# Gate and up by seven products: a pair of position chunks per weight block, even positions ahead of odd ones

## The chip, the cores and the metric

The kernel runs on one core of a Trainium2 chip. The metric is the device time of one execution in microseconds (us), lower is better. A core has five engines that run their own instruction streams and meet at semaphores: TensorE (PE: matmul, with weight loads, PEld, that overlap it), VectorE (DVE), ScalarE (ACT), GpSimd (POOL) and SyncE (SP, which here only issues transfers). Work is in SBUF (128 partitions); matmul results go to PSUM banks of 128 x 512 fp32, eight of them; DMA engines move data to and from HBM.

## The reference

Shapes: S = 2048 positions, D = 640, F = 1536, 32 heads of 20. All in fp32.

```python
xn = layernorm(x)                                    # no scale, no bias
q, k, v = (xn @ wqkv) split in 3, 32 heads of 20
# position s attends to s, s-2, ..., s-14: 8 places, every second one; before the start masked
A  = softmax(q.k * 20**-0.5) @ v, heads joined, @ wo
h  = (xn @ w_gate) * (xn @ w_up)                      # 2048 x 1536
out = x + A * silu(h @ w_down)
```

## The kernel before, in words

**Number format.** Each fp32 operand of a matmul is the sum of a high part (fp32 rounded to the matmul's fp32r format by an ACT copy) and a low part (what is left). A product is three matmuls: high by high, high by low, low by high. The low part comes either from a subtraction on DVE or POOL (`split`, L86 and L87), or without them (`split_dma`): ACT copies the high part (L91), ACT writes its negative into the low tile (L92), and a DMA that POOL issues adds the raw weights from HBM onto it (L93).

**Positions.** Since attention looks at every second position, positions are held as 16 tiles of 128, tiles 0 to 7 the even ones and 8 to 15 the odd ones; four tiles make a chunk of 512. Chunks 0 and 1 are even, 2 and 3 odd. The normalised, transposed input of all four chunks (high and low) stays in SBUF in four buffers `xc`.

**Gate and up.** F is 12 blocks of 128. For block f and chunk ch, `gate_up` runs 5 x 3 = 15 matmuls of 128 x 512 for gate into a PSUM bank `g`, 15 for up into `u` (L102), ACT copies the gate to SBUF (L435), DVE multiplies up by it (L446; the last 11 pairs by ACT and POOL, L448 and L449, when no attention is left on DVE), and SP stores the result to HBM (`h_scr`). There are 48 such pairs. The weight block f+1 is loaded by SP and split while the chunks of block f run.

**Attention.** The 32 heads are five groups of 6 or 7. A unit is a group at one parity, ten in all, group by group. A unit's q, k, v are 8 tiles x 15 matmuls of width 360 or 420 on PE (L327) that ACT moves out of PSUM (L329, L330). Its attention is all DVE work: 4 products q*k for two places at once (L363), 4 sums over a head (L367), softmax (its exponential on ACT, L379), 4 products with v (L388), 3 sums (L396) and a last one (L399). Each is one instruction of 1920 or 2240 elements per partition.

**Order.** The program is written in one order, and each engine runs its instructions in that order. `advance` puts DVE instructions of the attention between the rest: each matmul group on PE gives a credit of its own time (times `PACE`) that the next attention instructions use up. After the front (layernorm, transposes, unit 0, blocks 0 and 1 and unit 1) come units 2 to 9, with 2 to 4 gate/up pairs after each, then blocks 10 and 11 for all chunks, while the attention ends.

**After that.** `out_proj` for 16 tiles, each 30 matmuls of 320 wide (L102 into `q`), while the 12 blocks of `wd` are loaded, summed on DVE and split by ACT and POOL; `trans_o` (L507 and L87, all DVE) prepares each tile. Then the down projection: for 8 pairs of tiles 7 products of 18 matmuls of 320 wide (L646). These are already of the Strassen-Winograd kind: 7 half-size products of sums of quarters instead of 8, and where a result is wanted in two banks, ACT copies the bank to a second one, onto which later matmuls go on adding.

Of the kernel before, what the change touches and what calls it, by code (L numbers as in the profile page):

```python
# [42 lines left out]
PACE = 1.0  # L43
# [8 lines left out]
def kernel(  # L52
# [30 lines left out]

    def split(eng, raw, hi, lo):

        nc.scalar.activation(hi, raw, AF.Copy)  # L86
        eng.tensor_sub(lo, raw, hi.bitcast(F32))  # L87
# [17 lines left out]
    wq_raw, wq = {}, {}  # L105

    def load_wq(g, parts):
        c3 = 3 * GROUPS[g] * DH
        wq_raw[g] = []
        for p in parts:  # L110
            t = st([P, p[-1] - p[0], c3], "wraw", 3)
            for k0, k1 in zip(p, p[1:]):
                nc.sync.dma_start(t[:, k0 - p[0]:k1 - p[0]], wqkv[g][:, k0:k1, :])
                wq_raw[g].append((k0, k1, t[:, k0 - p[0]:k1 - p[0]]))

    def split_wq(g, eng, ks=(0, KD)):
        c3 = 3 * GROUPS[g] * DH
        if g not in wq:
            cp = -(-c3 // 64) * 64
            wq[g] = [st([P, KD, cp], tag, 1, F32R)[:, :, :c3] for tag in ("wqh", "wql")]  # L120
        for k0, k1, t in wq_raw[g]:
            if ks[0] <= k0 < ks[1]:
                if g:
                    split_dma(t, wqkv[g][:, k0:k1, :], wq[g][0][:, k0:k1], wq[g][1][:, k0:k1])
                else:
                    split(eng, t, wq[g][0][:, k0:k1], wq[g][1][:, k0:k1])

    wf_raw, wf = {}, {}

    def load_wf(f):  # L130
        wf_raw[f] = st([P, KD, 2, P], "wraw", 3)
        nc.sync.dma_start(wf_raw[f], wgu[f])

    def split_wf(f, eng, cuts=(0, KD)):
        hi, lo = st([P, KD, 2, P], "wf", 4, F32R), st([P, KD, 2, P], "wf", 4, F32R)
        if f > 1:
            split_dma(wf_raw[f], wgu[f], hi, lo)
        else:
            for k0, k1 in zip(cuts, cuts[1:]):
                split(eng, wf_raw[f][:, k0:k1], hi[:, k0:k1], lo[:, k0:k1])  # L140
        wf[f] = hi, lo


# [13 lines left out]
    load_wq(0, ((0, 1, 2, 3), (3, 4, 5)))  # L157
    load_x(2, 2, xe[:, 0:2])
    load_wf(0)
    xc = st([P, NE, D], "xc", NCH)  # L160
    load_x(4, 4, xc[:, 0:4])
    load_wf(1)
    load_x(8, 4, xc[:, 4:8])
    xd = st([P, 1, D], "o", 1)
    load_x(14, 1, xa[:, 2:3])
    load_x(15, 1, xd)
# [3 lines left out]
    def idle_product(n):  # L170

        nc.tensor.matmul(pt([P, n, P], "q", 4), ident, ident.unsqueeze(1).to_broadcast([P, n, P]), start=True,
                         stop=True)

    for n in (3, 3, 3, 2):
        idle_product(n)
# [3 lines left out]
    o_scr = dr.tile([DIL, NQ, NE, P, QC], F32, name="o_scr")  # L180
    h_scr = dr.tile([NT, P, KF, P], F32, name="h_scr")
    s_scr = dr.tile([NT, P, D], F32, name="s_scr")

    xT = []

    def xT_tile(s):
        if s % TPC == 0:
            y = st([P, 2, KD, CH], "xc", NCH, F32R)
            xT.append((y[:, 0], y[:, 1]))
        hi, lo = xT[s // TPC]  # L190
        c = (s % TPC) * P
        return hi[:, :, c:c + P], lo[:, :, c:c + P]

# [45 lines left out]
    def trans(s, later=False):  # L239
        hi, lo = xT_tile(s)  # L240
        for k0, k1 in ((0, 4), (4, KD)):
            p = pt([P, k1 - k0, P], "q", 4)
# [5 lines left out]
        if not later:  # L248
            low_parts()

# [19 lines left out]
    def spread(s):  # L270

        b = (s - FIRST) // 4
        p = pt([P, NQ, 2, 4], "q", 4)
# [3 lines left out]
    def trans_quarters(s):  # L277
# [3 lines left out]
        y = st([P, KD, P], "ot", 2)  # L281
        nc.vector.transpose(y.rearrange("p k (q i) -> p k q i", i=QB),  # L282
                            xt[s].rearrange("p (q k j) -> p k q j", q=NQ, j=QB))
        hi, lo = xT_tile(s)
        nc.scalar.activation(hi, y, AF.Copy)
        low_parts()
        halves.append(lambda: nc.vector.tensor_sub(lo, y, hi.bitcast(F32)))
# [8 lines left out]
    UN = [(g, r) for g in range(len(GROUPS)) for r in range(DIL)]  # L296
    q_t, kv_t, kv_buf, kv_zero = {}, {}, {}, {}

    def begin_unit(u, zero=True):
        g, r = UN[u]  # L300
        c = GROUPS[g] * DH
        q_t[u] = st([P, NE * CMAX + 32], "q", 2)[:, :NE * c].rearrange("p (i c) -> p i c", c=c)
        if r not in kv_buf:
            kv_buf[r] = st([P, EXT * 2 * CMAX], f"kv{r}", 1)
            kv_zero[r] = 0
        kv_t[u] = kv_buf[r][:, :2 * EXT * c].rearrange("p (a e c) -> p a e c", a=2, c=c)
        if zero:
            zero_front(u)

    def zero_front(u):  # L310
        g, r = UN[u]
        if kv_zero[r] != GROUPS[g]:
            nc.gpsimd.memset(kv_t[u][0:1, :, 0:W - 1, :], 0.0)
            kv_zero[r] = GROUPS[g]
# [3 lines left out]
    def qkv(u, i, runs=ALL_RUNS, at=None, act=None):  # L318
# [3 lines left out]
        p = pt([P, 3 * c], "q", 4)  # L322
        t0 = (i % TPC) * P
        for n, (a, b, k) in enumerate(runs):
            if n == at:
                act()
            nc.tensor.matmul(p, xT[(r * NE + i) // TPC][a][:, k, t0:t0 + P], wq[g][b][:, k], start=n == 0,  # L327
# [94 lines left out]
    def gate_up_half(f, ch, n, p, c=slice(0, CH), **parts):  # L422
        mm3(p[:, c], [([t[:, k, n, :] for t in wf[f]], [t[:, k, c] for t in xT[ch]]) for k in range(KD)], **parts)

    def gate_up(f, ch, between=(), amid=(), part=None):
# [5 lines left out]
        gate_up_half(f, ch, 0, pp[0], c)  # L431
# [4 lines left out]
        for act in between:  # L436
            act()
        share = (c.stop - c.start) / CH
        finish_piece()
        advance(PACE * 3.25 * share)  # L440
        gate_up_half(f, ch, 1, pp[1], c)

        def finish():
            hs = st([P, CH], "hs", 2)
            if running:
                nc.vector.tensor_mul(hs, pp[1], gs)  # L446
            else:
# [286 lines left out]
    for i in range(4):  # L734
        qkv(1, i)
# [173 lines left out]
```

## Time and profile before

| | us |
|---|---|
| runs (median of 3) | 770.22 (769.85 to 770.49) |
| profiled execution, its own time | 770.31 |
| its span in the trace | 768.5 |
| PE busy | 759.9 (99%) |
| DVE busy | 626.8 (82%) |
| ACT busy | 251.2 (33%) |
| POOL busy | 106.4 (14%) |
| bytes by DMA | 104.50 MB, 136 GB/s on average |

The span runs from the first to the last instruction in the trace; the execution's own time holds 1.81 us more. Busy shares are means over stages of unlike kind, so the stages are read apart: the front up to about 60 us, units and gate/up to 546, out projection to 616.4, down projection to the end.

### The profile page before, as it was taken

How to read it: one execution, taken by the hardware profiler on the slowest of the kernel's cores; microseconds unless marked ns; L12 is line 12 of the kernel's file. 1: busy time of each engine (PE TensorE's matmuls, PEld its weight loads, DVE VectorE, ACT ScalarE, POOL GpSimd, SP SyncE). 2: the span in 40 equal slices, each digit the busy share in tenths (PEclk: the TensorE clock that was granted, in tenths of full speed). 3: DMA queues.
4: the chain of work that ended last, by engine and by line, in shares of the span. 5: the costliest groups of instructions: out<-in, count | busy, mean ns of one | idle time of the engine just before them, and what ended most of it. 6: DMA issues, size and time to landing. Idle time of an engine off the chain costs nothing.

```text
span 768.5 us, 10609 instructions
## 1 busy us (share of the span) xinstructions
PE 759.9 (99%) x4192; PEld 700.5 (91%) x4192; DVE 626.8 (82%) x630; ACT 251.2 (33%) x520; POOL 106.4 (14%) x120
## 2 busy tenths in 40 slices
PE   8999999999999999999999999999999999999997
PEld 6989889999898998989889898888999999999997
DVE  6677999898999989989998999960377587777775
ACT  5323342113222132221412122213356554444442
POOL 7201011000100011010100000005377500000000
PEclk9999999999999999999999999999999999999999
DMA  8352185133643436235542422542887465555533
GB/s 327 145 171 87 40 210 118 53 106 104 118 108 84 140 72 135 74 67 150 111 95 86 87 88 66 176 100 72 209 244 209 168 250 183 186 187 185 185 104 137
DMA packets 82423, 104.50 MB, mean 136 GB/s; under 512 B 21101, under 2 KB 61901, under 8 KB 82117
## 3 DMA queue, kind: packets, MB, share of 16 engines
q1 hardware_dynamic: 72544, 84.16, 34.6%
q0 software_dynamic: 4128, 10.55, 8.1%
q10 hardware_dynamic: 5700, 9.11, 4.1%
q8 instruction: 33, 0.54, 0.3%
q14 instruction: 18, 0.14, 0.1%
HBM read 66.38 MB, written 28.31 MB: 123 GB/s over the span
## 4 chain that ended last, share of the span: by engine, by line
PE 93%; DMA 2%; DVE 2%; ACT 1%; ACTq 1%; issue 0%; POOL 0%; SPq 0%; POOLq 0%; DVEq 0%
PE q L327 24%; PE u L102 20%; PE g L102 20%; PE q L646 11%; PE q L102 9%; PE u L646 5%; PE g L646 3%; DMA wraw<-in_wgu 1%; DMA xc<-in_xq 1%; DVE xc L224 1%; ACTq L334 1%; DMA wraw<-in_wqkv 1%; DVE ot L282 0%; DVE stats L200 0%; POOL wql L87 0%
## 5 line engine op out<-in xcount | busy, mean ns | idle before, releaser
L102 PE MATMUL u<-xc,wf 128*128 128x512 f32 (+1 forms) x735 | 171.8, 386 | 0.0
L102 PE MATMUL g<-xc,wf 128*128 128x512 f32 (+1 forms) x735 | 171.8, 385 | 0.0
L102 PEld LDWEIGHTS u<-xc,wf 128*128 128x128 f32 x735 | 136.1, 188 | 27.3
L102 PEld LDWEIGHTS g<-xc,wf 128*128 128x128 f32 x735 | 136.0, 188 | 26.5
L327 PE MATMUL q<-wqh,xc 128*128 128x360 f32 (+1 forms) x800 | 152.9, 334 | 1.3 <-ACT xc L245 1.2
L327 PEld LDWEIGHTS q<-wqh,xc 128*128 128x128 f32 x800 | 138.3, 188 | 3.6 <-ACT xc L245 2.0
L388 DVE TENSOR_TENSOR t<-lg,kv 128x1920 f32<-128x1920 f32 (+1 forms) x40 | 90.8, 2288 | 0.8
L363 DVE TENSOR_TENSOR t<-q,kv 128x1920 f32<-128x1920 f32 (+1 forms) x40 | 90.9, 2287 | 0.5
L367 DVE TENSOR_REDUCE lg<-t 128x96 f32<-128x1920 f32 (+1 forms) x40 | 90.3, 2279 | 0.0
L327 PE MATMUL q<-wql,xc 128*128 128x360 f32 (+1 forms) x400 | 81.8, 334 | 0.0
L435 ACT ACTIVATE gs<-g 128x512 f32<-128x512 f32 x48 | 28.6, 595 | 160.3 <-PE g L102 156.4
L329 ACT ACTIVATE kv<-q 128x240 f32<-128x240 f32 (+1 forms) x80 | 30.9, 386 | 146.2 <-PE q L327 137.8
L327 PEld LDWEIGHTS q<-wql,xc 128*128 128x128 f32 x400 | 69.7, 188 | 0.1
L396 DVE TENSOR_TENSOR t<-t,t 128x1920 f32<-128x1920 f32 (+1 forms) x30 | 68.7, 2289 | 0.7
L646 PE MATMUL q<-xc,wf 128*128 128x320 f32 x432 | 67.3, 310 | 0.0
L646 PEld LDWEIGHTS q<-xc,wf 128*128 128x128 f32 x432 | 64.3, 188 | 0.0
L93 POOL DMA_DIRECT2D wf<-in_wgu x10 | 8.8, 882 | 242.0 <-ACT wf L92 242.0
L102 PE MATMUL q<-wf,wf 128*128 128x320 f32 x156 | 35.6, 310 | 0.0
L330 ACT ACTIVATE q<-q 128x120 f32<-128x120 f32 (+1 forms) x80 | 22.2, 277 | 14.2 <-DMA o_scr<-q 14.2
L102 PEld LDWEIGHTS q<-wf,wf 128*128 128x128 f32 x156 | 26.1, 188 | 0.0
L93 POOL DMA_DIRECT2D wql<-in_wqkv x8 | 10.0, 1246 | 115.1 <-ACT wql L92 114.6
L449 POOL TENSOR_TENSOR hs<-hs,gs 128x512 f32<-128x512 f32 x11 | 14.2, 1293 | 82.9 <-ACT hs L448 47.3
(166 smaller groups left out, 926.1 us busy)
## 6 DMA issues: line engine op xcount, KB each, us to landing
h_scr<-hs SPq DMA_DIRECT2D x48, 256.0 KB, 2.4
wraw<-in_wgu SPq DMA_DIRECT2D x12, 640.0 KB, 5.4
wf<-in_wgu POOLq DMA_DIRECT2D x10, 640.0 KB, 6.6
t<-h_scr SPq DMA_DIRECT2D x8, 768.0 KB, 7.7
hs<-s_scr SPq DMA_DIRECT2D x16, 320.0 KB, 3.5
gs<-in_x SPq DMA_DIRECT2D x16, 320.0 KB, 3.9
wraw<-h_scr SPq DMA_DIRECT2D x12, 384.0 KB, 6.0
out<-q SPq DMA_DIRECT2D x14, 320.0 KB, 2.5
```

What stands on the lines that cost most here:

```text
L93: nc.gpsimd.dma_start(lo, src, accum_op=ALU.add)
L102: nc.tensor.matmul(acc, a, b, start=first and n == 0, stop=last and n == len(runs) - 1)
L327: nc.tensor.matmul(p, xT[(r * NE + i) // TPC][a][:, k, t0:t0 + P], wq[g][b][:, k], start=n == 0, stop=n == len(runs) - 1, skip_group_check ...
L329: nc.scalar.activation(kv_t[u][:, :, W - 1 + i, :], p[:, c:].rearrange("p (a c) -> p a c", a=2), AF.Copy)
L330: nc.scalar.activation(q_t[u][:, i, :], p[:, :c], AF.Copy)
L363: nc.vector.tensor_mul(prods[j], q.rearrange("p i c -> p (i c)").unsqueeze(1).to_broadcast([P, 2, NE * c]), places(0, j))
L367: nc.vector.tensor_reduce(out=lg[:, :, j:j + 2].rearrange("p n a -> p a n"), in_=heads(prods.pop(j)), op=ALU.add, axis=AX.X)
L388: nc.vector.tensor_mul(heads(t), pw, heads(places(1, j)))
L396: nc.vector.tensor_add(acc, acc, t)
L435: nc.scalar.activation(gs, pp[0], AF.Copy)
L449: nc.gpsimd.tensor_mul(hs, hs, gs)
L646: nc.tensor.matmul(p, y[:, i, k], wd_t[name][k][:, l], start=new and r == 0, stop=r == len(runs) - 1, skip_group_check=True)
```

## The change

**Gate and up.** A job is now one block f for both chunks of one parity: 24 jobs, numbered 0 to 23. Four of them (f = 0 and 1 even, f = 11 even and odd) run as before, 15 + 15 matmuls for each chunk. The other 20 run as seven products. The weights of the block are taken as ten 128 x 128 pieces (5 of the inner dimension for gate, 5 for up), the positions as two chunks; four of the five inner pieces form 2 x 2 quarters, and the fifth is added where it belongs. The products have 6, 6, 6, 9, 9, 9 and 9 matmuls of 128 x 512: 54 where there were 60. Three banks hold the results: X (`g`, 2 buffers), V (`u`, 2) and Z (one bank, new, for which `q` gives up one of four). ACT copies X to Z after the first product, and both go on adding.

**Weight sums.** A job needs 16 pieces: 8 of the 10 raw ones and 8 sums. POOL makes the sums (4 instructions of 256 elements per partition) the first time a block is used as seven products, SP stores them to a new `w_scr`, and the second time (the other parity) loads them from there. All 16 pieces are split: 5 copies and 5 negations by ACT, and two DMAs that add, one from the raw weights and one from `w_scr`.

**Input sums.** The sums of the chunks are made once for each parity: for the even one on DVE in the front, for the odd one from HBM (`xt_scr`, to which the front stores the transposed odd tiles, and from which the odd chunks come back into SBUF, too). So only one parity is in SBUF at a time.

**Order.** Units are ordered by parity: 0 to 4 even, 5 to 9 odd. Since a group now comes twice, its qkv weights are loaded and split for every unit. `ORDER` gives the order of jobs (J) and units (U) after the front. A list of events with due times on a modelled PE clock (`later`, `step`, `need`) puts ACT, POOL, DVE and SP instructions between the matmuls.

**End.** `out_proj` of tiles 0 to 7 needs only even units, so the last odd attention may go on into it; `advance(1e9)` stands at s = 6. `trans_o` of tiles 1 to 5 uses ACT and an adding DMA for the low part. The loads, sums and splits of `wd` begin at s = 6, not s = 1.

```diff
-PACE = 1.0
+PACE = 1.02
+MM = 0.2267
+ORDER = "JJJJUJJJUJJUJJUJJUJJUJJUJJUJJJ"
...
+    UN = [(g, r) for r in range(DIL) for g in range(len(GROUPS))]
+    JOBS = [(f, 0, f in (0, 1, KF - 1)) for f in range(KF)]
+    JOBS += [(f, 1, f == KF - 1) for f in (KF - 1, *range(2, KF - 1), 0, 1)]
...
+        def sums():
+            done.add(("raw", i))
+            nc.gpsimd.tensor_sub(b[:, 2:4], a[:, 0:2], a[:, 8:10])
+            nc.gpsimd.tensor_add(a[:, 8:10], a[:, 8:10], a[:, 4:6])
+            nc.gpsimd.tensor_sub(b[:, 0:2], a[:, 8:10], a[:, 0:2])
+            nc.gpsimd.tensor_sub(b[:, 4:6], a[:, 2:4], b[:, 0:2])
+            nc.sync.dma_start(w_scr[f, :, :2], a[:, 8:10])
+            nc.sync.dma_start(w_scr[f, :, 2:], b)
...
+        for n, (k0, k1) in enumerate(cuts):
+            later(CHUNK * 2 * n, lambda k0=k0, k1=k1: high(k0, k1))
+            later(CHUNK * (2 * n + 1), lambda k0=k0, k1=k1: negate(lo[:, k0:k1], hi[:, k0:k1]))
+        later(CHUNK * 3 + 0.1, lambda: nc.gpsimd.dma_start(lo[:, :8], wgu[f, :, :8], accum_op=ALU.add))
+        later(CHUNK * 9 + 0.1, lambda: nc.gpsimd.dma_start(lo[:, 8:], w_scr[f], accum_op=ALU.add))
+        later(CHUNK * 9 + 0.1, lambda: done.add(("wf", i)))
...
+    def prod(p, i, terms, first=False):
+        w = wf[i]
+        runs = [(w[a][:, b], x[c][n]) for a, c in ALL3 for blocks, x in terms for n, b in enumerate(blocks)]
+        for n, (y, x) in enumerate(runs):
+            nc.tensor.matmul(p, y, x, start=first and n == 0, stop=n == len(runs) - 1, skip_group_check=True)
+        return len(runs) * MM
...
+    def strassen(i):
+        f, r, _ = JOBS[i]
+        need(("wf", i), f"xS{r}")
+        x = lambda name: xs(r, name)
+        X, Z, V = pt([P, CH], "g", 2), pt([P, CH], "z", 1), pt([P, CH], "u", 2)
+        t = prod(X, i, [((0, 1), x("B11"))], True)
+        copy(Z, X)
+        step(t)
+        t = prod(V, i, [((8, 9), x("T1"))], True)
+        m5 = copy(st([P, CH], "ot", 2), V)
+        step(t)
+        t = prod(X, i, [((10, 11), x("T2"))])
+        m = copy(st([P, CH], "hs", 2), X)
+        step(t)
+        t = prod(Z, i, [((2, 3), x("B21")), ((6,), x("A5"))])
+        gs = copy(st([P, CH], "gs", 2), Z)
+        step(t)
+        t = prod(X, i, [((12, 13), x("T3")), ((7,), x("B5"))])
+        w = copy(st([P, CH], "ot", 2), X)
+        nc.gpsimd.dma_start(w, m5, accum_op=ALU.add)
+        step(t)
+        t = prod(V, i, [((14, 15), x("B22")), ((6,), x("B5"))])
+        def upper():
+            nc.vector.tensor_add(m, V, m)
+        later(t + 0.3, upper)
+        step(t)
+        t = prod(X, i, [((4, 5), x("T4")), ((7,), x("D5"))])
+        def lower():
+            nc.vector.tensor_mul(gs, X, gs)
+        def both():
+            nc.vector.tensor_mul(m, m, w)
...
+        if s == 6:
+            begin_wd()
             load_wd(0)
+            load_wd(1)
             advance(1e9)
```

Three places of the instruction order follow, each before and in the change. A row gives the line, the operation, output and input by the program's names with a running number, and the shape.

**ACT while a weight block is split.** Before, the two rows of 1280 stand between the gate copies (`gs`) of one block's pairs:

```order
L435 ACTIVATE gs_3053<-g_3036 128x512
L435 ACTIVATE gs_3089<-g_3072 128x512
L91 ACTIVATE wf_3091<-wraw_3034 128x1280
L92 ACTIVATE wf_3092<-wraw_3034 128x1280
L435 ACTIVATE gs_3134<-g_3117 128x512
L435 ACTIVATE gs_3178<-g_3161 128x512
```

In the change, inside one job of seven products (L252 a high part, L155 a negation of the next job's weights, L760 a bank that is copied):

```order
L252 ACTIVATE wf_3041<-wraw_3007 128x512
L760 ACTIVATE ot_3068<-u_3045 128x512
L155 ACTIVATE wf_3042<-wf_3041 128x512
L252 ACTIVATE wf_3041<-wraw_3007 128x256
L760 ACTIVATE hs_3080<-g_3043 128x512
L155 ACTIVATE wf_3042<-wf_3041 128x256
L252 ACTIVATE wf_3041<-wraw_3008 128x384
L760 ACTIVATE gs_3095<-z_3044 128x512
L155 ACTIVATE wf_3042<-wf_3041 128x384
L252 ACTIVATE wf_3041<-wraw_3008 128x384
L155 ACTIVATE wf_3042<-wf_3041 128x384
L760 ACTIVATE ot_3113<-g_3043 128x512
```

The split of the next block is now cut into ten pieces between the copies of the running job, and three of them stand behind the copy of Z (`gs` from `z`), which waits for the fourth product.

**POOL over a few jobs.** Before, POOL has only the adding DMAs there (`wql` the low part of qkv weights, `wf` of gate/up weights):

```order
L313 MEMSET kv_102_753 1x2x980
L93 DMA wql_1689<-in_wqkv 128x3x420
L93 DMA wql_1689<-in_wqkv 128x2x420
L93 DMA wf_1716<-in_wgu 128x1280
L93 DMA wf_2053<-in_wgu 128x1280
```

In the change, two jobs long:

```order
L274 DMA wf_1729<-in_wgu 128x1024
L275 DMA wf_1729<-w_scr 128x1024
L783 DMA ot_1793<-ot_1750 128x512
L228 TENSOR_TENSOR wraw_1797<-wraw_1796 128x256
L229 TENSOR_TENSOR wraw_1796<-wraw_1796 128x256
L230 TENSOR_TENSOR wraw_1797<-wraw_1796 128x256
L231 TENSOR_TENSOR wraw_1797<-wraw_1796,wraw_1797 128x256
L274 DMA wf_1833<-in_wgu 128x1024
L275 DMA wf_1833<-w_scr 128x1024
```

The sums of a job's weights (L228 to L231) now stand directly ahead of the two DMAs of the same job's split (L274, L275), and behind the DMA that adds one product onto another (L783).

**DVE at the end of the attention.** Before, the last attention instruction (L399) stands ahead of the first preparation of a tile for `out_proj` (L507, L87):

```order
L396 TENSOR_TENSOR t_3914<-t_3914,t_3913 128x1920
L399 TENSOR_TENSOR q_3544<-t_3914 128x960
L507 STREAM_TRANSPOSE ot_4205<-wraw_3943 128x640
L87 TENSOR_TENSOR kv_497_4207<-ot_4205,kv_497_4207 128x640
L507 STREAM_TRANSPOSE ot_4266<-o_4210 128x640
```

In the change (L667 and L659 are the lines that were L396 and L388, L670 was L399, L843 was L507):

```order
L667 TENSOR_TENSOR t_4809<-t_4809,t_4808 128x1920
L659 TENSOR_TENSOR t_4808<-lg_4546,kv_109_776 128x1920
L843 STREAM_TRANSPOSE xa_4876<-xa_4772 128x640
L667 TENSOR_TENSOR t_4809<-t_4809,t_4808 128x1920
L659 TENSOR_TENSOR t_4808<-lg_4546,kv_109_776 128x1920
L843 STREAM_TRANSPOSE xa_4921<-xa_4772 128x640
L667 TENSOR_TENSOR t_4809<-t_4809,t_4808 128x1920
L670 TENSOR_TENSOR q_4287<-t_4809 128x960
L843 STREAM_TRANSPOSE ot_5002<-xa_4772 128x640
L126 TENSOR_TENSOR wf_5004<-ot_5002,wf_5004 128x640
```

Transposes for `out_proj` now stand between the attention's last instructions, and the one for tile 6 (`ot_5002`) with its low part behind all of them.

More of the change, by code (lines that the diff above doesn't have):

```diff
@@ L128 @@
[L128 to L141, printed above, removed]
+        cp = -(-c3 // 64) * 64
@@ L469, in gate_up_first @@
             for n in range(2):
-                gate_up_half(f, ch, n, pp[n], slice(0, CH // 2), parts=parts, first=first, last=not first)
+                gate_up_half(i, ch, n, pp[n], slice(0, CH // 2), parts=parts, first=first, last=not first)
             if first:
@@ new lines @@
+    at, u = 2, 2
+    for what in ORDER:
+        if what == "U":
+            unit(u)
+            u += 1
+        else:
+            job(at)
+            at += 1
+    load_o(4, 4, st([P, 4, D], "xa", 4))
+    finish_piece()
+    trans_o(1)
+    n_prod = 7 * NT // 2
+    items, at = [divmod(n, 2) for n in range(2 * KH)], 0
+    for s in range(NT):
+        if s + 2 < AHEAD_O:
+            trans_o(s + 2)
+        elif AHEAD_O <= s + 1 < NT:
+            trans_o(s + 1)
+        if s == 6:
+            begin_wd()
+            load_wd(0)
+            load_wd(1)
+            advance(1e9)
+            load_o(8, 3, st([P, 3, D], "t", 2))
+        if s in (8, 10):
+            load_o(*((11, 3) if s == 8 else (14, 2)), st([P, 3 if s == 8 else 2, D], "t", 2))
+        now = items[at:max(0, (s - 6) * 2 * KH // 8)]
+        at += len(now)
+        for k, part in now:
```

600 lines of the change are left out of this document (425 added, 175 removed).

## The prediction

> **What bounds the kernel now.** I read the page first: busy times, the slices, the chain that ended last.
>
> ```profile
> span 768.5 us, 10609 instructions
> PE 759.9 (99%) x4192; PEld 700.5 (91%) x4192; DVE 626.8 (82%) x630; ACT 251.2 (33%) x520; POOL 106.4 (14%) x120
> ...
> DVE  6677999898999989989998999960377587777775
> ...
> PE 93%; DMA 2%; DVE 2%; ACT 1%; ACTq 1%; issue 0%; POOL 0%; SPq 0%; POOLq 0%; DVEq 0%
> ```
>
> PE is 99% busy and holds 93% of the chain. DVE is nearly full from slice 5 to slice 26, about 86 to 512 us, so a shorter PE stage there may uncover it. Next the busy times by stage (us, PE, PEld, DVE, ACT, POOL, then clock, DMA share, GB/s):
>
> ```profile
> 0.00:60.00 60.00, 55.66 (x299) 48.00 (x300) 42.82 (x125) 22.45 (x60) 20.40 (x42) 1.00 0.60 207
> 60.00:86.50 26.50, 26.50 (x141) 23.97 (x141) 21.36 (x53) 8.94 (x21) 4.02 (x3) 1.00 0.21 70
> 86.50:240.00 153.50, 153.50 (x756) 139.99 (x755) 147.33 (x95) 41.19 (x88) 10.88 (x9) 1.00 0.44 109
> 240.00:400.00 160.00, 160.00 (x802) 143.21 (x801) 150.44 (x92) 39.28 (x82) 10.82 (x10) 1.00 0.44 107
> 546.00:616.40 70.40, 70.40 (x482) 70.40 (x481) 45.23 (x56) 38.71 (x91) 43.06 (x43) 1.00 0.75 210
> 616.40:768.50 152.10, 147.80 (x1008) 147.54 (x1006) 112.38 (x139) 67.62 (x113) 0.00 (x0) 0.99 0.51 179
> ```
>
> From 60 to 616 us PE never waits, at the full clock (1.00). ACT has three quarters of its time free between 86 and 400 us, DMA more than half. So the time is the number of matmuls by what one takes. What one takes, from the timeline and the chain (start, length, rows):
>
> ```profile
> 501.61 3.56 PE L102 MATMUL u<-xc,wf 128*128 128x512 f32 x15
> 505.00 3.56 PE L102 MATMUL g<-xc,wf 128*128 128x512 f32 x15
> ...
> 305.97 19.20 PE q L327 x120
> 545.97 70.39 PE q L102 x480
> 743.08 5.28 PE q L646 x36
> ```
>
> Fifteen 512-wide matmuls repeat every 505.00 - 501.61 = 3.39 to 3.40 us, 0.2267 us each. `out_proj` starts at 545.97.
>
> **What PE saves.** Each of 20 jobs has 54 matmuls for 60: 120 fewer, 120 x 0.2267 = 27.2 us. That holds only if adding products to one bank, or to a bank that ACT has filled, costs PE nothing. The down projection does both already: 36 of its matmuls take 5.28 us, 0.1467 each, like `out_proj` (70.39 / 480 = 0.1467), which does neither. So span 768.5 - 27.2 = 741.3 if nothing new is waited for. A job is 54 x 0.2267 = 12.24 us, and gate/up would end at 545.97 - 27.2 = 518.8. Below, waits are added to that.
>
> **ACT.** Rows for its work on weights and banks:
>
> ```profile
> L435 ACT ACTIVATE gs<-g 128x512 f32<-128x512 f32 x48 | 28.6, 595 | 160.3 <-PE g L102 156.4
> L91 ACT ACTIVATE wf<-wraw x10: 1259/1267/1274, 94.9 to 495.6; 128x1280 fp32r<-128x1280 f32 x10
> ```
>
> A 512-wide copy is 0.60, a 1280-wide 1.27; by the line through them 256 is 0.37 and 384 is 0.48. A job's five copies out of PSUM take 3.0, the ten split pieces 2 x (2 x 0.60 + 0.37 + 2 x 0.48) = 5.1: 8.1 of 12.24 us, so ACT is no bound. The copy X to Z must end before Z is added to, two products (12 matmuls, 2.7 us) later, and the copies of X have at least 9 matmuls (2.0 us) before X is written again; 0.60 fits in each, with one split piece ahead of it too. I take 0; each 0.6 us not covered would cost 20 x 0.6 = 12. The qkv weights are now split for every unit, ten ACT pieces of about 0.5 us each, and stand among the copies out of a job's or a unit's banks, which may start a piece late: I take 2 us in all, 0 to 5.
>
> **(a) The second adding DMA.** It is issued when the last negation is done. In the order of ACT three pieces stand behind the copy of Z, which starts after 6 + 6 + 6 + 9 = 27 matmuls, 6.1 us into the job. So 6.1 + 0.6 + 3 x 0.48 = 8.2 us. The rows for how long such a DMA takes to land:
>
> ```profile
> wf<-in_wgu POOLq DMA_DIRECT2D x10, 640.0 KB, 6.6
> DMA to landing us min/median/max: 6.0/6.6/9.9
> q0 software_dynamic: 4128, 10.55, 8.1%
> ```
>
> 8.2 + 6.6 = 14.8. The next job first reads a low part from the second half in the last two matmuls of its second product (ten matmuls in, 2.27 us): at 12.24 + 2.27 = 14.5 if it follows directly. That is 0.3 us late, and with 6.0 not late, with 9.9 it is 3.6 late. Twelve of the transitions between jobs have no unit between them; at the others a unit's 19.2 us cover it. The bytes by order of the program rise from 104 to 165 MB and those that add from 10.55 MB to some 42, so I put the landing 0.3 us above the median: 0.6 x 12 = 7 us. Bounds 0 and 3.6 x 12 = 43. Landings before ran from 6.0 to 9.9, with the median near the low end, so the value lies near that end.
>
> [...]
>
> **(b) POOL's sums.** Eleven blocks get four 256-wide sums on POOL. Their nearest rows (the 256-wide POOL subtractions of the front; a POOL and a DVE subtraction that met in `out_proj`):
>
> ```profile
> L87 POOL TENSOR_TENSOR wf<-wraw,wf x12: 721/740/1571, 13.5 to 529.1; 128x256 fp32r<-128x256 f32 x10, 128x640 fp32r<-128x640 f32 x2
> L87 DVE TENSOR_TENSOR wf<-ot,wf x13: 824/826/1487, 549.4 to 601.6; 128x640 fp32r<-128x640 f32 x13
> 557.47 0.88 POOL L87 TENSOR_TENSOR xc<-lg,xc 128x320 fp32r<-128x320 f32 x1
> 557.54 1.49 DVE L87 TENSOR_TENSOR wf<-ot,wf 128x640 fp32r<-128x640 f32 x1 [0.87 <-ACT wf L86]
> ```
>
> Alone a sum is 0.74, four 3.0 us. But the DVE subtraction that began at 557.54, 0.07 us after POOL's of 0.88, took 1.49 for 0.826: it lost 0.66 of the 0.81 left of POOL's. So the two wait for each other. Where a DVE product of attention goes first, POOL may wait 2.16 per sum: four sums 11.6 us at most. ACT's high parts of the summed pieces wait for them, behind these the split's DMAs and SP's stores to `w_scr`, and behind those SP's next weight load. In four places (jobs 4, 5, 8 and 23) sums are due just before the split. I take 1.5 us for each, 6 in all, between 0 and 7 each.
>
> **(c) DVE.** The attention's first and last rows, the next work, and what else stands among it:
>
> ```profile
> 86.52 4.22 DVE L363 TENSOR_TENSOR t<-q,kv 128x1920 f32<-128x1920 f32 x2
> 510.50 1.16 DVE L399 TENSOR_TENSOR q<-t 128x960 f32<-128x960 f32 x1
> 538.50 0.84 DVE L507 STREAM_TRANSPOSE ot<-wraw 128x640 f32<-128x640 f32 x1 [26.84 <-DMA wraw<-o_scr]
> L446 DVE TENSOR_TENSOR hs<-u,gs 128x512 f32<-128x512 f32 x37 | 25.3, 683 | 0.3 <-issue 0.3
> ```
>
> From 86.5 to 511.7 are 425.1 us; less the 37 products of 25.3 that is 399.8 for the attention with its short waits. In the change DVE has in this stretch 20 x 3 instructions for the jobs (41.0), 4 for the plain pairs, 9 for the sums of the odd input (13 x 0.683 = 8.9) and six transposes of 0.84 (5): 399.8 + 41.0 + 8.9 + 5 = 454.7, so 86.5 + 454.7 = 541.2. In the front DVE loses eight low parts and gains eight sums and nine low parts, which I put at even. 36 of POOL's 44 sums fall in this stretch; if all hit DVE they cost 36 x 0.74 = 26.6, and I take half, 13: 554.5. Tile 6 of `out_proj` needs a transpose and a low part after that (1.7): 556.2. PE would get there at 518.8 + 6 x 4.4 = 545.2 (a tile is 30 x 0.1467). So DVE sets a floor of 11 us of waits. It is not added to PE's own, since PE's waits earlier give DVE time; the larger counts. The wd splits that now wait until s = 6 (43.06 busy on POOL above, of 70.4) have from about 556 to the end of `out_proj` at 741.3 - 152.1 = 589.2 plus the waits: with 16 us of waits 605, a little over 43 us. That gives about the same floor, some 10.
>
> **Front (e).** The split of the second group's qkv weights comes a unit earlier: 1 us, 0 to 3.
>
> **Sum.** 27.2 saved; waits 7 (a) + 6 (b) + 2 (units' weights) + 1 (e) = 16, above the floor of 11. Span 768.5 - 27.2 + 16 = 757.3. The profiled execution took 770.31 for a span of 768.5, 1.8 more, and lies within 0.1 of the median, so **759** for the run.
>
> **Rivals.**
> - *R1, full gain.* The landings stay near 6.0 us, POOL's sums find gaps of DVE. (a), (b) fall to nothing, DVE still has to reach tile 6 about when PE does (541.2 + 1.7 = 542.9 for 545.2 with no lock at all). Waits 2 to 5: 745 to 748. For it: DMA was 44% busy, ACT has a third free. Against: doubled load of DMA, landings up to 9.9 already.
> - *R2, POOL and DVE.* Every sum costs DVE its 0.74: 541.2 + 26.6 + 1.7 = 569.5 against 545.2, 24 us: span 765.6, run 767. For it: DVE is full there (147.33 of 153.50). Against: a DVE instruction that runs first makes POOL wait instead. [...]
> - *R3, the other side: preparing weights is slower than PE.* Each job needs its pieces loaded, added in two halves and the sums stored or loaded. At 44% of the DMA engines and 109 GB/s before, 165 MB in 750 us would be 220 GB/s, and 210 GB/s took 0.75 (stage 546). Then adding DMAs land later, and every job waits. It decides from 27.2 / 20 = 1.36 us a job. With landings at 8.2 in place of 6.6, (a) is 1.9 x 12 = 23, and with 10 for (b) and the rest 33: span 774.5, run 776. If also jobs beside a unit wait (the queue never empties), 780. For it: before, the same kind of DMA took up to 9.9. Against: stage 546 to 616 runs at 0.75 and PE did not wait.
> - *R4, seven products are not cheaper on PE* (a bubble where products change bank, 0.19 us at each of 7 x 20 changes would eat the gain): 770. Against it is the row at 743.08.
>
> **How the numbers follow.** Chances: forecast 0.50 (its own range 750 to 766), R1 0.20, R2 0.13, R3 0.15, R4 0.02. No change is within 0.2%, 768.7 to 771.8, about what a measurement here can tell. Faster: 0.50 + 0.20 + about half of R2 (0.06) = 0.76. Within 0.2%: the upper end of R2, R4 and the low end of R3, 0.07. Slower: 0.17. The range is 745 to 774: R1 from its lower end, forecast and R2 whole, R3 only at its foot.
>
> **What would show it.** Right: about 120 rows fewer than 4192 on PE, 54 per job in 12.24 us; seven-product jobs whose idle time before the second or third product ends on the adding DMA from `w_scr`, 0.3 to 1 us each and only where job follows job; a median landing of 6.6 to 7; four larger gaps at jobs 4, 5, 8 and 23 that end on ACT, and behind it POOL's sums; DVE's last attention row near 550 to 556; out projection's matmuls waiting less than 3 us at tile 6 in all. Wrong: matmuls of a job over 0.2267 (R4); landings over 8 us and waits beside units too (R3); PE waiting ten us or more at tile 6 with DVE still at attention (R2); no waits (R1). The forecast falls if PE's new waits from 86 us to the end of gate/up sum to under 8 or over 25.

## The result, and the profile after

The changed kernel took 861.32 us (median of 4 runs, 857.36 to 864.59) against 770.04 us before: a ratio of 1.118, 95% interval 1.113 to 1.123. It is 91 us slower; 759 with a range of 745 to 774 had been forecast.

The page of the changed kernel, its span, busy times, the clock granted to TensorE in 40 slices, and three rows of DMAs that add (name, count, size, median us from issue to landing):

```profile
span 857.8 us, 11177 instructions
PE 779.1 (91%) x4072; PEld 696.9 (81%) x4072; DVE 671.7 (78%) x670; ACT 399.4 (47%) x877; POOL 230.0 (27%) x242
PEclk9999798899999999899999999998998999999999
...
wf<-in_wgu POOLq DMA_DIRECT2D x21, 512.0 KB, 8.1
wf<-w_scr POOLq DMA_DIRECT2D x20, 512.0 KB, 8.5
...
ot<-ot POOLq DMA_DIRECT2D x20, 256.0 KB, 9.1
```

PE has 120 rows fewer, as it should, yet is busy 19 us longer (759.9 before) and idle 70 us longer (78.7 for 8.6). The clock is no longer full everywhere. The adding DMAs of the gate and up weights, which took 6.6 us to land, take 8.1 and 8.5, and the new ones that add one product onto another (`ot`) take 9.1.

By stage, before (first two rows) and after (last two): the units with gate and up from 83.3 us on, and the out projection. Columns as in the prediction: length, busy PE, PEld, DVE, ACT, POOL, then clock, DMA share, GB/s.

```profile
83.30:546.00 462.70, 462.70 (x2287) 413.60 (x2286) 408.03 (x265) 114.74 (x238) 38.95 (x32) 1.00 0.41 104
546.00:616.40 70.40, 70.40 (x482) 70.40 (x481) 45.23 (x56) 38.71 (x91) 43.06 (x43) 1.00 0.75 210
```

```profile
83.30:607.50 524.20, 475.80 (x2179) 404.68 (x2178) 427.18 (x306) 248.39 (x567) 147.48 (x139) 0.96 0.82 196
607.50:703.60 96.10, 76.34 (x481) 73.96 (x479) 64.15 (x60) 42.59 (x93) 48.53 (x47) 0.95 0.66 178
```

The first stage, which should have become 27 us shorter, is 61.5 us longer, 48.4 of it idle PE. The out projection, whose matmuls did not change, is 25.7 us longer. The rest adds 2.1: 89.3 us of span in all. What PE waited for (us in total, times, longest):

```profile
PE u L756 <- DMA wf<-w_scr: 16.3, 9, 4.5
PE g L756 <- DMA wf<-in_wgu: 12.8, 7, 5.0
PE q L141 <- ACT gs L869: 8.6, 5, 2.3
PE g L756 <- ACT hs L760: 7.3, 2, 5.1
PE q L141 <- ACT wf L125: 4.9, 1, 4.9
PE q L141 <- DMA xb<-xa: 4.5, 1, 4.5
PE q L598 <- ACT q L601: 3.6, 2, 2.9
PE g L756 <- ACT z L760: 3.6, 3, 2.1
```

Weights that land late (`wf`) are 29.1 us; banks that ACT copies late, about 16 (`hs`, `z`, `q`, and 1.8 us for `ot`, not shown); in the out projection (L141) another 18.

**A wait costs more than its length.** PE's timeline where one job follows another (start, length, rows, the wait ahead of it), and the stretches around it with the granted clock (third column from the right):

```profile
122.62 1.07 PE L756 MATMUL g<-xa,wf 128*128 128x512 f32 x4
127.63 1.22 PE L756 MATMUL g<-xa,wf 128*128 128x512 f32 x2 [3.93 <-DMA wf<-in_wgu]
128.65 1.91 PE L756 MATMUL u<-xb,wf 128*128 128x512 f32 x4
```

```profile
120.00:123.70 3.70, 3.70 (x16) 2.65 (x15) 2.74 (x6) 1.06 (x2) 1.39 (x2) 1.00 1.07 206
126.60:133.20 6.60, 5.37 (x12) 3.78 (x13) 0.64 (x2) 2.01 (x4) 1.26 (x2) 0.50 0.72 164
133.40:140.00 6.60, 6.60 (x30) 5.25 (x28) 6.53 (x3) 4.53 (x11) 6.34 (x4) 1.00 0.08 27
```

Late in a wait of 3.93 us the clock falls to 0.50, for 6.8 us (126.55 to 133.37), and the two matmuls behind it take 1.02 us in place of 0.45. Such stretches of 3.4 or 6.8 us sum to 58 us of this execution (before: none from 60 to 616 us). Matmuls fill 49 us of them, at half rate, so some 25 us are lost on top of the waits (an estimate from these two numbers).

### The profile page after: what moved, and what is told of

Its sections match the earlier page's. It is cut to its first block, busy times and chain, and to the rows that moved or that the text cites. A ratio compares the mean times of both kernels' runs of the same rounds, so it can differ in the third digit from the quotient of the medians.

```text
span 857.8 us, 11177 instructions
## 1 busy us (share of the span) xinstructions
PE 779.1 (91%) x4072; PEld 696.9 (81%) x4072; DVE 671.7 (78%) x670; ACT 399.4 (47%) x877; POOL 230.0 (27%) x242
## 5 line engine op out<-in xcount | busy, mean ns | idle before, releaser
L756 PE MATMUL g<-xa,wf 128*128 128x512 f32 x312 | 92.5, 411 | 11.6 <-DMA wf<-in_wgu 10.6
L756 PE MATMUL g<-xb,wf 128*128 128x512 f32 x288 | 87.3, 415 | 13.8 <-ACT hs L760 7.3
L659 DVE TENSOR_TENSOR t<-lg,kv 128x1920 f32<-128x1920 f32 (+1 forms) x40 | 91.9, 2316 | 0.9
L756 PEld LDWEIGHTS g<-xa,wf 128*128 128x128 f32 x312 | 59.8, 196 | 29.2 <-DMA wf<-in_wgu 11.8
L598 PE MATMUL q<-wqh,xa 128*128 128x360 f32 (+1 forms) x400 | 80.5, 344 | 3.3 <-DVE xa L556 2.0
L598 PE MATMUL q<-wqh,xb 128*128 128x360 f32 (+1 forms) x400 | 80.0, 344 | 2.9 <-ACT q L601 2.9
L756 PEld LDWEIGHTS g<-xb,wf 128*128 128x128 f32 x288 | 55.5, 197 | 30.9 <-ACT hs L760 8.6
L598 PEld LDWEIGHTS q<-wqh,xb 128*128 128x128 f32 x400 | 72.0, 193 | 4.6 <-ACT q L601 3.2
L598 PEld LDWEIGHTS q<-wqh,xa 128*128 128x128 f32 x400 | 71.0, 191 | 5.6 <-DVE xa L556 2.3
L667 DVE TENSOR_TENSOR t<-t,t 128x1920 f32<-128x1920 f32 (+1 forms) x30 | 71.0, 2365 | 0.8
L274 POOL DMA_DIRECT2D wf<-in_wgu x20 | 18.7, 935 | 181.6 <-ACT wf L252 180.8
L252 ACT ACTIVATE wf<-wraw 128x512 fp32r<-128x512 f32 (+2 forms) x100 | 53.7, 537 | 9.2 <-DMA wraw<-in_wgu 6.0
L155 ACT ACTIVATE wf<-wf 128x512 fp32r<-128x512 f32 (+2 forms) x103 | 55.7, 543 | 3.0 <-DMA hs<-in_xq 1.6
```

The costliest lines, as they stand in the source:

```text
L155: nc.scalar.activation(lo, hi.bitcast(F32), AF.Copy, scale=-1.0)
L252: nc.scalar.activation(hi[:, k0:k1], raw, AF.Copy)
L274: later(CHUNK * 3 + 0.1, lambda: nc.gpsimd.dma_start(lo[:, :8], wgu[f, :, :8], accum_op=ALU.add))
L659: nc.vector.tensor_mul(heads(t), pw, heads(places(1, j)))
L667: nc.vector.tensor_add(acc, acc, t)
L756: nc.tensor.matmul(p, y, x, start=first and n == 0, stop=n == len(runs) - 1, skip_group_check=True)
```

## The experiments

The kernels from e1 on were timed beside the kernel before (769.8 to 770.1). Medians are of runs, stages of the profiled execution; idle is PE's.

| kernel | median us | from 83.3 to out projection (idle) | out projection |
|---|---|---|---|
| before | 770.0 | 462.7 (0) | 70.4 |
| the change | 861.3 | 524.2 (48.4) | 96.1 |
| e1_align | 850.3 | 509.2 (44.2) | 98.8 |
| e2_no_add | 819.4 | 481.3 (21.0) | 96.4 |
| e3_no_m5 | 854.7 | 518.9 (44.6) | 98.8 |
| e4_no_sums | 844.7 | 506.2 (41.9) | 99.3 |
| e5_shift32 | 859.7 | 522.4 (52.5) | 98.0 |
| e6_no_prep | 792.6 | 458.0 (11.9) | 95.4 |
| e7_no_last_attention | 857.1 | 521.5 (57.5) | 98.1 |
| e8_order_alone | 900.8 | 557.6 (64.3) | 100.1 |
| e9_order_alone2 | 822.7 | 480.1 (12.9) | 102.1 |
| e10_no_wd_sums | 838.6 | 517.4 (50.1) | 84.8 |
| e11_early_odd | 843.4 | 512.5 (47.7) | 90.2 |
| e12_plain_loads | 833.8 | 490.9 (30.9) | 98.8 |

Runs of one kernel that waits much scatter by up to 10 us (e1: 848.2 to 857.6), so differences of that size are read from the traces, not from the medians.

### e1: where the tiles start

PE's timeline of the changed kernel shows one more thing: two plain jobs (15 + 15 matmuls for each chunk) that follow each other, the first with its moving operand in xa, the second in xb.

```profile
310.02 3.56 PE L141 MATMUL g<-xa,wf 128*128 128x512 f32 x15
313.42 3.56 PE L141 MATMUL u<-xa,wf 128*128 128x512 f32 x15
316.82 3.67 PE L141 MATMUL g<-xb,wf 128*128 128x512 f32 x15
320.33 3.68 PE L141 MATMUL u<-xb,wf 128*128 128x512 f32 x15
```

Fifteen matmuls from xa take 3.40 us, as before, from xb 3.51, without a wait and at full clock. The units take 23.2 and 19.8 us for 22.4 and 19.2. In the built program xa, wf and all that lies behind kv0 start 32 bytes off a multiple of 64; xb and the qkv weights do not, and before the change no large tile did.

```diff
     for r in range(DIL):
         st([P, EXT * 2 * CMAX], f"kv{r}", 1)
-        st([P, 24], f"gap{r}", 1)
+        if r:
+            st([P, 24], f"gap{r}", 1)
```

> The gap of 96 bytes behind the first kv buffer is dropped. In the change that buffer is itself 96 bytes longer than before, so that kv1, q, xa, wf, gs, hs and ot start 32 bytes off a multiple of 64; without the gap all start at multiples of 64 again, as before the change. Placement theory (the 2 to 4% that a matmul reading xb or wqh takes longer, 234 ns for 227, 165 for 160, come from operands that lie 32 bytes apart from each other): these matmuls go back to 227, 160 and 187 ns, PE busy falls by some 13 us, and the time by 13 to 15 us, to about 847. Rival (they come from the heavier traffic of other engines and DMA in that stage, not from where a tile starts): the matmul times stay, the time stays at 857 to 865.

Measured: 850.3. The same place of its timeline:

```profile
302.20 3.56 PE L141 MATMUL u<-xa,wf 128*128 128x512 f32 x15
305.60 3.56 PE L141 MATMUL g<-xb,wf 128*128 128x512 f32 x15
309.00 3.56 PE L141 MATMUL u<-xb,wf 128*128 128x512 f32 x15
```

3.40 us for all, and between starts the medians are 227, 160 and 187 ns again. So the placement did slow the matmuls, for these went back while the traffic of the other engines stayed. The time is 11 us less by the medians, 11.4 by the spans, a little under the 13 to 15 expected, and no more than the scatter of the runs; the matmul times are what shows the cause.

### e5: what about the placement

```diff
-    st([P, 32], "skip", 1)
+    st([P, 40], "skip", 1)
```

(on top of e1).

> The gap behind the first kv buffer is dropped as in e1_align, and 32 bytes are put ahead of all tiles, so that every large tile starts 32 bytes off a multiple of 64, t, xb, wqh and wql too. If what slows a matmul is that the tiles in use lie 32 bytes apart from each other modulo 64: all are alike again, 227, 160 and 187 ns, time like e1_align (848 to 852). If it is that a tile starts off a multiple of 64 at all: more matmuls are slow than in the change, at 234, 165 and 193 ns, and the time is 860 or more.

Measured: with every large tile 32 bytes off, the medians are 227, 160 and 187 ns as in e1. So what slowed them here is not that a tile starts off a multiple of 64, but that the tiles are unlike. The time, 859.7, does not show it: this kernel waited 8 us more than e1 before the out projection (52.5 idle for 44.2) and had more of half clock there (44.4 us for 37.5). Which pair of tiles has to be unlike stays open: in the change the odd units, which read only xb and the qkv weights, both at multiples of 64, were slow as well.

### e2, e3, e4, e6: preparing the weights

```diff
e2:
-        later(CHUNK * 3 + 0.1, lambda: nc.gpsimd.dma_start(lo[:, :8], wgu[f, :, :8], accum_op=ALU.add))
-        later(CHUNK * 9 + 0.1, lambda: nc.gpsimd.dma_start(lo[:, 8:], w_scr[f], accum_op=ALU.add))
e3:
-        nc.gpsimd.dma_start(w, m5, accum_op=ALU.add)
e4:
+        nc.sync.dma_start(b, wgu[f, :, :6])
...
-            nc.gpsimd.tensor_sub(b[:, 2:4], a[:, 0:2], a[:, 8:10])
-            nc.gpsimd.tensor_add(a[:, 8:10], a[:, 8:10], a[:, 4:6])
-            nc.gpsimd.tensor_sub(b[:, 0:2], a[:, 8:10], a[:, 0:2])
-            nc.gpsimd.tensor_sub(b[:, 4:6], a[:, 2:4], b[:, 0:2])
e6: e1 + e2 + e3 + e4
```

> The two adding DMAs on POOL that complete the low parts of a job's weights are left out, so the low parts stay the negative of the high parts; everything else is issued as in the change. Late-weights theory (the adding DMAs, landing after 8 us and more, are what jobs wait for): the waits of PE for wf (29 us) go, most of the 20 us of half clock between 86 and 607 us go with them, and since the queue is shorter the other adding DMAs land near 6 us: 800 to 815 us. Rival (blocked engines: ACT held up by buffers, sums and copies is what makes the jobs late, the DMAs only come last): waits for the copies of ACT take the place of those for wf, and no more than 15 us are won: 845 or more.

> The adding DMA that adds the second product onto the third bank's copy (on POOL, 20 times 256 KB) is left out, so half of the upper result lacks one product. Blocked-engines theory (this DMA, landing after 9 us, holds the two ot buffers; ACT waits for them with the copies of the next job behind it, and DVE waits 32 us for it): the waits of ACT for ot (11.5 us) go, landings of the weights' adding DMAs fall by 0.5 to 1 us, 10 to 20 us are won: 840 to 850. Late-weights theory: only the shorter queue counts, 3 to 8 us: 852 to 858.

> POOL's four sums per block are left out; the six pieces of sums are loaded from the raw weights instead (another 384 KB for each of 11 blocks), everything else is as in the change. If late sums are what holds ACT and POOL in the even half (jobs 2 to 11, with 20 of PE's idle us before 303 us): 15 to 25 us are won, nearly all before 303 us: 835 to 847. If the sums are covered and the adding DMAs alone are late: within 5 us of the change, with the odd half unchanged in both cases.

> With the gap dropped as in e1_align, all that e2, e3 and e4 leave out is left out together: both adding DMAs of each split, the adding DMA of the second product, POOL's sums (their pieces are loaded raw). If preparing weights and the engines that it blocks are the whole loss of the gate/up stage: that stage takes 435 to 450 us (54 matmuls a job, no waits over 1 us), the stage of out projection stays at 97, and the time is 782 to 797, still over 770. If DVE or the copies of ACT bound the seven products too: waits for ACT remain and the stage takes 465 or more: 810 and up.

Measured, e2: 819.4 without the weights' adding DMAs, 42 us less than the change and 4 above the 800 to 815 of the late-weights theory. The waits for wf are gone, idle time fell from 48.4 to 21.0 us, half clock in the stage from 44.4 to 10.2. The other theory (at most 15 us) falls.

e3: 854.7 without the second product's DMA, some 7 us and within the scatter. It fits the late-weights figure (852 to 858), not that of blocked engines.

e4: 844.7 without POOL's sums, 17 us, and the gain is made before 303 us, as the first theory had it. It comes mostly through the clock: half clock 17.1 us for 44.4, idle only 6.5 less. PE still waits 23.3 us for wf, but in pieces of at most 2.3 us where the change has waits of up to 5.0.

e6: with all this and the gap left out, the stage takes 458.0 us, over the 435 to 450 expected, and 11.9 us of it are still idle. The time is 792.6, in its range, and still over the kernel before. e6 keeps ACT's ten pieces for each block and SP's loads and stores, so not every cost of preparing weights is out of it; but without adding DMAs and sums the change still loses.

How a late weight comes about shows where one job follows another in the odd half. POOL's issues, then PE; the first job began at 412.26, the next at 425.01.

```profile
418.13 0.86 POOL L274 DMA_DIRECT2D wf<-in_wgu  x1 [29.72 <-ACT wf L252]
421.50 0.89 POOL L275 DMA_DIRECT2D wf<-w_scr  x1 [2.51 <-DVE t L667]
422.50 0.87 POOL L783 DMA_DIRECT2D ot<-ot  x1
```

```profile
426.31 0.74 PE L756 MATMUL g<-xb,wf 128*128 128x512 f32 x2 [0.21 <-DMA wf<-in_wgu]
426.88 1.09 PE L756 MATMUL u<-xa,wf 128*128 128x512 f32 x4
429.73 0.73 PE L756 MATMUL u<-xa,wf 128*128 128x512 f32 x2 [1.76 <-DMA wf<-w_scr]
```

The first adding DMA is issued 5.9 us into the job and lands 8.1 us later, when the next job's first product already waits for it; the second is issued at 9.2 us, with the third right behind it, lands after 8.2, and the second product waits. In the even half POOL's sums stand ahead of both:

```profile
111.09 2.69 POOL L228 TENSOR_TENSOR wraw<-wraw 128x256 f32<-128x256 f32 x1
113.86 1.08 POOL L229 TENSOR_TENSOR wraw<-wraw 128x256 f32<-128x256 f32 x1
115.01 0.74 POOL L230 TENSOR_TENSOR wraw<-wraw 128x256 f32<-128x256 f32 x1
115.83 0.74 POOL L231 TENSOR_TENSOR wraw<-wraw,wraw 128x256 f32<-128x256 f32 x1
```

Four sums, 0.74 each where nothing is in the way, took 5.5 us, the first 2.69: DVE had begun a product of 2.15 us at 111.04, just ahead of it. The two DMAs behind them landed after 10.3 and 11.1 us, and PE waited the 3.93 us shown above.

### e12: adding, or only loading

```diff
-        nc.gpsimd.dma_start(lo[:, :8], wgu[f, :, :8], accum_op=ALU.add)
+        nc.gpsimd.dma_start(lo[:, :8], wgu[f, :, :8].bitcast(F32R))
-        nc.gpsimd.dma_start(lo[:, 8:], w_scr[f], accum_op=ALU.add)
+        nc.gpsimd.dma_start(lo[:, 8:], w_scr[f].bitcast(F32R))
```

(on top of e1; its low parts are the raw weights).

> With the gap dropped as in e1_align, the two DMAs of each split are issued by POOL as before with the same bytes, but write the raw weights over the low parts instead of adding them. If adding is what makes these DMAs slow: they land after 4 to 5.5 us, PE's waits for wf (28 us) fall below 8, and the time is 815 to 830. If it is POOL's queue or the traffic on the DMA engines: landings stay at 7.5 us or more, and the time is 843 to 853.

From issue to landing for all DMAs into wf, in the change, in e1 and in e12:

```profile
DMA to landing us min/median/max: 5.5/8.4/14.6
```

```profile
DMA to landing us min/median/max: 5.9/8.6/14.8
```

```profile
DMA to landing us min/median/max: 3.5/6.2/11.4
```

833.8, between the two expectations. Adding costs some 2.4 us of a landing (8.6 in e1, 6.2 in e12), and waits for wf fall from 25.3 us to 9.7. What makes up the other 6.2 us, POOL's queue or the traffic, was not tried apart.

### e8, e9: the order alone

```diff
-    JOBS = [(f, 0, f in (0, 1, KF - 1)) for f in range(KF)]
-    JOBS += [(f, 1, f == KF - 1) for f in (KF - 1, *range(2, KF - 1), 0, 1)]
+    JOBS = [(f, 0, True) for f in range(KF)]
+    JOBS += [(f, 1, True) for f in (KF - 1, *range(2, KF - 1), 0, 1)]
...
-    raw_sums(y4)
...
e9 only, in load_wf (a job ahead):
+        nc.sync.dma_start(a, wgu[f])
...
```

> With the gap dropped as in e1_align, all 24 jobs are plain (60 matmuls, two products, no sums of inputs or weights, three high parts and two adding DMAs per split), in the order of the change: even units first, qkv weights per unit, odd input loaded again, out projection and down weights as in the change. If the new order is itself costly: the gate/up stage is like that of before (463 us) plus some waits, the stage of out projection stays at 95 to 99, and the time is 795 to 810. If the order is free and the seven products are the whole loss: 768 to 775.

> As e8_order_alone (all 24 jobs plain, order of the change, gap dropped), but the raw weights are loaded a job ahead and high parts and negations are issued from the start of a job on, as the change does for its seven-product jobs. e8 lost 64 us to waits, most of them 4 to 7 us at each job that follows a job, because its weights were only loaded at the start of the job before. If that was its fault and not the order's: these waits fall below 1 us each, the gate/up stage takes 465 to 480 us, the out projection stays at 95 to 100, and the time is 795 to 815. If the order itself (qkv weights per unit, odd input loaded again, both beside the jobs' weights) keeps the adding DMAs late: waits of 2 to 4 us at job after job remain, 830 or more.

e8 did not answer its question: it loaded its weights only when the job ahead began, its twelve waits for them come to 52.6 us, and it took 900.8. e9 has that mended: two waits for weights are left (4.7 us), and the time is 822.7. Its stages:

```profile
83.30:563.40 480.10, 467.21 (x2285) 412.46 (x2283) 415.10 (x282) 175.66 (x409) 83.72 (x74) 0.99 0.66 157
563.40:665.50 102.10, 83.89 (x480) 81.28 (x480) 53.77 (x54) 42.46 (x94) 48.60 (x47) 0.87 0.60 165
```

So with the same number of matmuls as before (PE busy 467 for 462.7) the order costs 53 us: 17 up to the out projection, and 32 in it. Order here means all that the change does beside the seven products: qkv weights for every unit, nearly every block split twice, the odd input loaded again, and the later down weights; these were not tried apart. The time lies between the two expectations: the first stage is that of the theory that e8's fault was its own, but for two waits that are left, and the out projection is dearer than expected. And from e9 to e1 (850.3) the seven products add another 28 us instead of taking 27.

### e7, e10, e11: the out projection

```diff
e7, in attention(u): for the last unit, q is stored and nothing computed
e10:
-            split(nc.gpsimd, wd_v[k][name], *(wd_t[name][k][:, i] for i in range(2)))
+            nc.scalar.activation(wd_t[name][k][:, 0], wd_v[k][name], AF.Copy)
+            nc.gpsimd.memset(wd_t[name][k][:, 1].bitcast(F32), 0.0)
     (and no sums in sum_wd)
e11:
+        if s == 4:
+            advance(1e9)
+            load_o(8, 3, st([P, 3, D], "t", 2))
         if s == 6:
...
-            advance(1e9)
-            load_o(8, 3, st([P, 3, D], "t", 2))
```

(all on top of e1).

> With the gap dropped as in e1_align, the attention of the last unit is left out (its q is stored as its output), so DVE is free some 40 us earlier. If the attention that ends late on DVE is what makes the stage of out projection 27 us too long: the wait at tile 6 (6 us) and those behind it go, the stage falls from 99 to 75 to 80 us, and the time to 828 to 835. If the splits of the down weights, pressed into tiles 6 to 15, are the cause: only the wait at tile 6 with its half clock goes, the stage stays above 88, 838 to 846.

> With the gap dropped as in e1_align, the sums of the down weights on DVE are left out and POOL's subtractions for their low parts are replaced by fills with zero, which read nothing. If the down weights, pressed into eight tiles, make the out projection long (POOL and DVE waiting for each other, ACT behind them with the copies that PE waits for): the waits of PE for ACT's copies from tile 9 on (about 10 us with their half clock) go, the stage falls from 99 to 83 to 88 us, the time to 835 to 840. If those waits are set by the out projection's own loads: the stage stays above 94, 845 or more.

> With the gap dropped as in e1_align, the rest of the attention and the load of the first three odd tiles' outputs are written at tile 4 of the out projection, not at tile 6. Nothing is left out. If the wait of 5 to 6 us ahead of tile 8 comes from that load standing late in SP's queue (it was issued some 10 us after the attention had ended): the wait falls to 0 to 2 us and one period of half clock goes, 6 to 9 us are won: 841 to 845. If it comes from the attention: it stays, or moves, 848 to 853.

e7 gained nothing (857.1, in the scatter): its wait of 4.8 us ahead of tile 8 is still there, so the attention does not set it. What does is in the change's own DVE and SP rows: the attention's last instruction, SP's store of its output and its load for tiles 8 to 10, and the transpose that waits for them.

```profile
627.48 1.16 DVE L670 TENSOR_TENSOR q<-t 128x960 f32<-128x960 f32 x1
```

```profile
632.52 0.37 SPq L675 DMA_DIRECT2D o_scr<-q  x1
636.49 0.32 SPq L871 DMA_DIRECT2D s_scr<-gs  x1
640.89 0.32 SPq L871 DMA_DIRECT2D s_scr<-hs  x1
641.30 1.86 SPq L897 DMA_DIRECT2D wraw<-in_wd  x4
643.22 2.04 SPq L836 DMA_DIRECT2D t<-o_scr  x4
```

```profile
652.35 0.84 DVE L843 STREAM_TRANSPOSE ot<-t 128x640 f32<-128x640 f32 x1 [10.00 <-DMA t<-o_scr]
654.08 0.90 PE L141 MATMUL q<-wf,wf 128*128 128x320 f32 x2 [4.91 <-ACT wf L125]
```

The output was ready at 628.6; SP, in the program's order behind the stores of each finished tile, stored it at 632.5 and loaded it again from 643.2 on. e11 writes both earlier: the wait ahead of tile 8 is gone, the stage is 8.6 us shorter (90.2), and the median 843.4, as expected. e10 takes away the waits for ACT's copies from tile 9 on: the stage falls to 84.8, 14 us less, the median to 838.6, as its first theory had it. So of the 26 to 28 us, about 14 come from summing and splitting the down weights, which now stand beside eight tiles and not twelve, 9 from that load, and most of the rest from one wait of 4.5 to 5.3 us at tile 1, for the adding DMA that makes its low part (`xb<-xa`), with the half clock after it; that one was not tried apart.

None of these leads to a kernel that beats the one before. Even e6, without adding DMAs and sums, stands at 792.6; if the 14 and 9 us that e10 and e11 won in the out projection could be had in it as well (no run shows that), it would come to about 770, the time of before.

## Why the prediction was wrong

The step that failed is the sum of the waits. It put 16 us on top of the matmuls' time. The trace has 70 us more of idle PE, 48 of them between 83.3 us and the end of gate and up, where the forecast itself set 25 as its limit; on top come some 25 us at half clock and some 11 by the placement of tiles.

- **PE's saving was right**: 54 matmuls a job. Six jobs of e6 take 12.24 us each, as forecast; those of e1 and e6 that have no wait over 0.3 us take 12.2 to 12.7. So adding onto banks that already hold something costs PE nothing of note (R4 falls).
- **(a) failed by its size.** The mechanism was right: it is R3, which had 0.15, with its landing of 8.2 us (median 8.4). R3 priced (a) at 23 us with that landing, and in e4, where no sums stand in the way, PE waits 23.3 us for wf. The forecast took 6.9, from a queue with one such DMA at a time; now three follow each other within 4.4 us, and DMA is busy 0.82 of the time for 0.41. It also costed only the second DMA, issued at 8.2 us (9.2 in the trace); the first is late too. 7 us were forecast, the waits for wf in the change, (b)'s among them, are 29, and leaving these DMAs out won 42.
- **(b) named the right places, jobs 4, 5, 8 and 23** (waits at 123.7, 144.0 with 147.4, 217.3 and 589.4 us), but at 1.5 us each, where PE waited 3.7 to 6.2. Together that is 18.7 of the 29 us: the waits end on the adding DMAs, not on ACT as forecast. POOL held up beside DVE is in it: 2.69 us for a sum that takes 0.74 elsewhere, with a DVE product of 2.15 begun just ahead. e4 puts the sums at 17 us.
- **ACT was put at 2 us, on the ground that it is busy 8.1 of a job's 12.24 us.** PE waited some 16 us for its copies. ACT had the time, but stands in one order: once it waited 8.9 us for an ot buffer whose store was under way, with the copies for the job behind.
- **The clock was not in the sum at all**: 58 us at half clock, some 25 us lost. The trace of before, in which PE never waited between 60 and 616 us, had no row for it. In the change half clock came in stretches of 3.4 or 6.8 us. Over ten traces it followed 18 of 33 waits of 2 to 3 us and 59 of 62 longer ones, but only 13 of 171 shorter ones (below). So waits of the lengths forecast, 0.6 and 1.5 us, would have drawn little of it; those that came, up to 5.1 us in this stage, drew much.
- **The order was taken as free but for 3 us (units' weights and front)**; it cost 53 (e9), 32 of them in the out projection. There the forecast read DVE's floor and the later wd splits, put both at 10 to 11 us, and added neither, since the other waits were larger. DVE's floor was right and did not bind: the attention ended 21 us after the out projection began (forecast: 554.5, with gate and up ending at 518.8 + 16 = 534.8, so 20), and e7 shows that it held nobody, so R2 falls. The wd sums and splits alone were worth 14 (e10). What else held PE was SP's order (e11) and, not tried apart, a low part by DMA at tile 1.
- **The placement (11 us)** hangs on one line of the whole diff, which is not among those shown: `z = st([P, 2 * EXT * CMAX + 24], "kv0", 1, F32R)` makes the first kv buffer 96 bytes longer, and all that lies behind moves. No row of the trace of before could have priced it.

One way to add it up: 770 became 823 by the order, 850 with the seven products, and 861 with the placement; the 27 us that PE saved are inside the second step. What in the order cost the 17 us ahead of the out projection stays open.

## What to carry to other kernels

Where an engine runs without a single wait, a change that saves it a few per cent must be costed with the price of waits that it has never shown: here waits of 3 to 4 us had 4.6 us at half clock with them in the mean, longer ones 6.2, so another 2 to 3 us lost (an estimate: half of that time). What is taken off the bound engine and given to queues that were half idle has to arrive within the shorter stage; cost each transfer at the load the change makes, not at the one it finds, and count every transfer that the next stage reads. And a change of order is a change of its own: time it alone.

## What was not expected of the hardware

The clock after a wait, counted over ten traces (before, the change, e1 to e8; waits of PE from 80 us to the start of the down projection). A wait counts as followed when a stretch at half clock begins during it or up to 3.4 us behind it.

| wait us | waits | followed by half clock | mean us at half clock |
|---|---|---|---|
| 0.3 to 1 | 71 | 1 | 0.0 |
| 1 to 2 | 100 | 12 | 0.5 |
| 2 to 3 | 33 | 18 | 2.1 |
| 3 to 4 | 18 | 16 | 4.6 |
| 4 and more | 44 | 43 | 6.2 |

Some of these waits follow each other closely. Of those with no other wait within 6.8 us, 2 of 19 of 1 to 2 us and 7 of 12 of 2 to 3 us were followed by half clock, so a wait of 2 us alone can be enough. What decides between those that were and those that were not stays open.

And in the change, where some large tiles start 32 bytes off a multiple of 64 and others do not, matmuls that read xb or the qkv weights took some 3% longer at full clock: 234 ns for 227, 165 for 160, 193 for 187. With all large tiles alike, at 0 (e1) or at 32 (e5), they took 227, 160 and 187 ns. Matmuls of 320 columns took 147 ns in all four kernels (before, the change, e1, e5).
